# A retention block and a three-way maxout feed-forward on one core: the order of weight conversion, transposes and weight sums between the matmuls

## The chip, the cores and the metric

The kernel runs on one core of a Trainium2 chip. The metric is the device time of one execution in microseconds (us), as a median over several executions. The core has five engines, each of which works through its own instruction queue: TensorE (PE in the profile, with its weight loads as PEld), VectorE (DVE), ScalarE (ACT), GpSimd (POOL) and SyncE (SP). SyncE only issues DMAs here.

## What is computed

The reference, cut to what matters:

```python
# attention: batch 8, heads 8, sequence 576, head dimension 64, float32
scores = scale * np.matmul(q, k.transpose(0, 1, 3, 2))
gamma = 1.0 - 2.0 ** (-5.0 - np.arange(H, dtype=np.float32))
Dmat = np.where(rel >= 0, gamma[:, None, None] ** rel[None, :, :], 0.0)
attn = np.matmul(scores * Dmat, v)                       # rel = i - j
x = attn.transpose(0, 2, 1, 3).reshape(4608, 512)
# feed-forward: d_model 512, d_ff 768, weights given in float64
h = np.maximum(np.maximum(x @ w1, x @ w2), x @ w3)
out = h @ w_out
```

## The kernel before, in words

The 4608 tokens are cut into 36 chunks of 128 tokens, and four chunks make a block t of 512 tokens; there are nine blocks, 0 to 8. Attention is done chunk by chunk in its recurrent form: per chunk the kernel transposes q and k (`transposes`), multiplies them into scores and masks these (`scores`), multiplies keys by decayed values into a state (`state`, scaled and added in `keep`), and multiplies scores and old state with values and queries into the chunk's output (`values`, whose last step `output` writes xT, the transposed input of the feed-forward). Chunks up to 6 are transposed on TensorE and copied by ScalarE (L274, L275); from chunk 7 on VectorE transposes them (`kT`, `qT`, through `soon`).

The feed-forward of block t (`ffn(t)`) runs while the attention of block t+1 is woven into it: `steps(t+1)` is a list of twelve slots written out by hand, and the main loop does one slot's steps and then lets the feed-forward go on to its next `yield`.

The weights come in float64. `convert_all` is a generator that turns them into float32 with integer operations on VectorE and ScalarE. Each unit of two 128-row pieces goes through `exponent` (L632 on VectorE, L634 on ScalarE), `fraction` (L640, L641, L643), `whole` (L646), `sign` (L650) and `product` (L658), which writes the float32 weight and issues the load of a further piece on SyncE. `convert(n)` advances the generator by n of its stops. Units 0 to 2 go half by half; from unit 3 on both halves go together, and the exponent of unit n+1 comes ahead of the sign and product of unit n.

Block 0 uses the plain products: `up_plain` (L786) for each of three weight matrices and six 128-row groups of the hidden layer, in the order of `units`, which is three entries (matrices) for each pair fp of groups; then `downs_plain` (L773). The queue of VectorE is in the order of these calls, so `convert(n)` and the attention steps share it in the order in which they stand in the code.

Blocks 1 to 8 use a scheme with fewer multiplications. For each pair fp of hidden groups, a "hidden pair" (order 0, 2, 1), `up` (L762) makes 20 products of sums of x and sums of weights, accumulated in five matmul banks a to e; `after` copies them on ScalarE (L747, `part` or `h`) and joins them on VectorE (L750). A join is a sum or maximum; those named D2, B6 and A7 come three at a time at the end of a hidden pair. The sums of weights are made once in place, 19 per hidden pair (`weight_sums`, L470). The sums for pair 0 are made at the end of block 0, those for pairs 2 and 1 during block 1. `downs` (L559) is the output stage in seven products with the matrices T (from sums of the output weights) and S (hidden sums, `sums_of_hidden`: two on VectorE, L527 and L528, two on GpSimd, L529). The profile calls the first, third, fifth and seventh product dx, the second dy, the fourth and sixth dz; `To` are the buffers t1, t2 and t4 of the output weights' sums, and the fourth product (dz) uses b12, which is changed in place in `w_out`.

In blocks 1 to 8 two lists feed VectorE's queue between the matmuls: `urgent` (steps of the attention, the hidden sums, the loads; `soon` appends to it) and `chores` (weight sums). `chore(n)` takes n from `urgent`, or from `chores` if `urgent` is empty. Before the scores or values of a chunk everything in `urgent` is taken. In `ffn`, one of two branches is taken after each of the 40 steps of a hidden pair (L866 to L869): every fourth step takes one of `urgent` (also two steps later if `urgent` is long), and even steps take one of `chores`.

The lines that matter below: L203 (masks, xT and transposes that are done at once, without the list; the same at L196 from the list), L310 and L313 (scores sk and states kv of a chunk from 8 on), L345 (`state_factors`, a copy on ScalarE whose result GpSimd reads in L327), L512 and L513 (sums of the output weights on VectorE), L516 and L517 (the same on GpSimd), L880 (where these are put in the queues), L919 to L934 (the attention of block 0, in the order written out by hand).

Of the kernel before, what the change touches and what calls it, by code (L numbers as in the profile page):

```python
# [45 lines left out]
ALU = mybir.AluOpType  # L46
# [17 lines left out]
            b21 = b21 - b41, b42 = b42 - n5, b22 = b22 - b21, n6 = b31 + n2, b32 = b22 - b32, n8 = b12 - n4,  # L64
# [17 lines left out]
def kernel(  # L82
# [14 lines left out]
    nc = tc.nc  # L97
# [8 lines left out]
    CPT = NT // C  # L106
# [150 lines left out]
    def transposes(g):  # L257
        both = qks[g] = {}
        if g >= BY_CHUNKS:
            for n, tag in (("k", "kT"), ("q", "m1")):  # L260
                both[n] = att.tile([P, H, D], FP32, tag=tag, name=n + "T", bufs=2 if n == "k" else 3)
        else:
            both["k"] = att.tile([P, NP, C], FP32, tag="kT", name="kT", bufs=2)
            both["q"] = ppool.tile([P, NP, C], FP32, tag="part", name="qT")
        if g >= BY_PE:
            for n in ("k", "q"):
                soon(partial(nc.vector.transpose, both[n][:].rearrange("a p c -> a (p c)"),
                             raws.pop(("kx" if n == "k" else n, g))[:].rearrange("a x y i -> a (x y i)")))
            return
        for n, src in (("k", raws["k", g]), ("q", raws.pop(("q", g)))):  # L270
            pool, tag = (ps_r, "r") if g >= CPT else (ps_x, "x")
            pt = pool.tile([P, NP, C], FP32, tag=tag, name=n + "t")
            for p in range(NP):
                nc.tensor.transpose(pt[:, p, :], pair(src, p), ident[:C, :C])  # L274
            nc.scalar.copy(both[n][:], pt[:])  # L275

    def scores(g):
        chore(len(urgent))
        scale(len(scaling))
        if g >= BY_CHUNKS:  # L280
            chunk_scores(g)
            return
        qT, kT = qks[g]["q"], qks[g]["k"]
        s = [ps_r.tile([C, NP, C], FP32, tag="r", name=f"s{j}") for j in range(2)]
        for p in range(NP):
            for j in range(2):
                r = slice(D * j, D * (j + 1))
                nc.tensor.matmul(s[j][:, p, :], lhsT=kT[r, p, :], rhs=qT[r, p, :], start=True, stop=True)
        for j in range(2):
            st = sts[g, j] = att.tile([C, NP, C], FP32, tag=f"m{j}", name="st", bufs=2 + j)  # L290
            soon(partial(nc.vector.tensor_tensor, st[:], s[j][:],
                         masks[start_of(g)][:].unsqueeze(1).to_broadcast([C, NP, C]), op=ALU.mult))
# [50 lines left out]
    def state_factors():  # L343
        for j in range(2):
            nc.scalar.copy(gs_of[half(0), j::2], gs[half(j)])  # L345

    def state(g):

        kr = raws["k", g]
        kvs[g] = None  # L350
        if begins(g):
            r = start_of(g) or 0
            kvs[g] = ps_r.tile([P, NP, D], FP32, tag="r", name="kv")
            for h in range(H):
                nc.tensor.matmul(kvs[g][half(h % 2), h // 2, :], lhsT=kr[r:, h, :], rhs=vds[g][r:, h, :],
                                 start=True, stop=True)

    def keep(g):
        factor = gs[:].unsqueeze(2).to_broadcast([P, NP, D])

        def step(t, kv):
            if start_of(g) is not None:
                nc.vector.tensor_tensor(t[:], kv[:], factor, op=ALU.mult)
            else:
                nc.vector.tensor_tensor(t[:], kv[:], states[g][:], op=ALU.add)
                (nc.gpsimd if g < CPT - 2 else nc.vector).tensor_tensor(t[:], t[:], factor, op=ALU.mult)

        if begins(g):
            t = states[g + 1] = ppool.tile([P, NP, D], FP32, tag="part", name="state")
            soon(partial(step, t, kvs[g]))  # L370
# [133 lines left out]
    def sums_of_outs():  # L504

        pool = late["pool"]
        lo, hi = slice(0, DM // 2), slice(DM // 2, DM)
        b11, b12, b21, b22 = (w_out[:, :, e, r] for e in range(2) for r in (lo, hi))
        t1, t2, t4 = (pool.tile([P, NF // 2, DM // 2], FP32, name=f"To{n}")[:] for n in (1, 2, 4))

        def on_vector(fp):
            nc.vector.tensor_tensor(t1[:, fp], b12[:, fp], b11[:, fp], op=ALU.subtract)  # L512
            nc.vector.tensor_tensor(t2[:, fp], b22[:, fp], t1[:, fp], op=ALU.subtract)  # L513

        def on_gpsimd(fp):
            nc.gpsimd.tensor_tensor(b12[:, fp], b22[:, fp], b12[:, fp], op=ALU.subtract)  # L516
            nc.gpsimd.tensor_tensor(t4[:, fp], b21[:, fp], t2[:, fp], op=ALU.subtract)  # L517

        late["sums of T"] = [partial(on, fp) for on in (on_vector, on_gpsimd) for fp in (0, 2, 1)]
        late["T"] = {1: b11, 2: b21, 3: b22, 4: t4, 5: t1, 6: t2, 7: b12}  # L520
        late["S"] = {n: pool.tile([P, NF // 2, NH], FP32, name=f"H{n}") for n in (1, 2, 3, 4)}

# [201 lines left out]
    def late_room():  # L724
        pool = late["pool"]
        late["W"] = [pool.tile([P, NF, P], FP32, name=f"n{n}") for n in range(1, 9)]
        late["X"] = {n: pool.tile([P, NH], FP32, name=n)[:] for n in sorted({x[0] for x in X_SUMS})}
# [3 lines left out]
    def convert(n):  # L731
        for _ in range(n):
            next(converting, None)
# [84 lines left out]
    def ffn(t):  # L818

        h = hpool.tile([P, NF, NT], FP32, tag="h", name="h")  # L820
        if t == 0:
            for fp, i in units:
                if (fp, i) == units[0]:
                    first_ups(h)
                    yield
                    continue
                for fb in (2 * fp, 2 * fp + 1):
                    maximum, = up_plain(t, h, fb, i)
                    if (fp, i, fb) == (*units[1], 0):
                        scores(CPT)  # L830
                        state(CPT)
                        keep(CPT)
                    if (fp, i) == units[-1] and fb % 2:
                        maximum()
                        convert(2)
                    else:
                        convert(4 if (fp, i) == units[1] else 2)
                        maximum()
                yield
            convert(3)  # L840
            for fb, _ in enumerate(downs_plain(t, h)):
                convert(2 if fb < 2 else 4 * len(pieces))
                if fb == 2:
                    while_converting.close()
                    late["pool"] = ctx.enter_context(tc.tile_pool(name="late", bufs=1))
                    late_room()
                    sums_of_outs()
                    weight_sums(0)
                elif fb == 3:
                    chore(len(chores))  # L850
                if fb in (1, 3):
                    yield
            yield
            return
        order = (0, 2, 1)
        if t == 1:
            spread.append(True)
            weight_sums(2)
            weight_sums(1)
        total = len(order) * 2 * len(PRODUCTS)  # L860
        count = parts = 0
        for fp in order:
            while fp not in summed_fp:
                chore()
            for step, _ in enumerate(up(t, h, fp)):
                if step % 4 == 1 or step % 4 == 3 and len(urgent) > (2 if t == 1 else 6):  # L866
                    chore(len(urgent) > 0)
                elif step % 2 == 0 and chores:
                    chores.popleft()()  # L869
                if step % 3 == 2:  # L870
                    scale()
                count += 1
                if count * (NF // 2 * 3) >= (parts + 1) * total:
                    parts += 1
                    yield
            sums_of_hidden(h, fp)
        chore(len(urgent))
        for n, _ in enumerate(downs(t, h, order)):
            if t == 1 and n == 0:
                for step in late["sums of T"]:  # L880
                    step()
            chore(4)
            scale(2)
            if n in (1, 3):
                yield
        yield
# [34 lines left out]
    decay(2)  # L921
    state(1)
    keep(1)
    values([1], [1])
    scores(2)
    convert(2)
    state(2)
    keep(2)
    convert(1)
    values([2], [2])  # L930
    transposes(CPT - 1)
    convert(1)
    state_factors()
    convert(2)  # L934
    decay(CPT - 1)
    scores(CPT - 1)
# [99 lines left out]
```

## Time and profile before

| | value |
|---|---|
| median of 3 executions | 753.45 us (753.13 to 753.48) |
| profiled execution: time, and span in the profile | 753.01 us, 751.3 us |
| TensorE busy | 743.1 us (99% of the span) |
| TensorE weight loads busy | 615.1 us (82%) |
| VectorE busy | 518.7 us (69%) |
| ScalarE busy | 327.3 us (44%) |
| GpSimd busy | 71.4 us (10%) |
| DMA | 59.31 MB, 79 GB/s over the span, 232 GB/s over the first 60 us |
| TensorE clock granted | 1.0 |

Busy times are of one profiled execution; the end of a matmul is modelled, so a busy TensorE is not TensorE at its peak, and a short wait can hide in a modelled end. In time the span falls into three stretches: attention of block 0 with the first weights (to about 22 us), block 0's plain feed-forward beside the conversion (to 123.81 us, where block 1's first matmul e starts), and blocks 1 to 8, of which block 1 still makes sums of weights. The loads are crowded at the start: the first 60 us move 13.94 MB of the 59.31.

### The profile page before, as it was taken

What the parts mean: (1) busy time and instruction counts of PE and PEld (TensorE: products, weight loads), DVE (VectorE), ACT (ScalarE), POOL (GpSimd) and SP (SyncE); (2) the same over time, 40 slices, a digit from 0 to 9 for tenths busy, and PEclk for the clock granted to TensorE, in tenths of its full rate; (3) what the DMA queues carried; (4) which work ended last, traced back from release to release, by engine and by line L of the source; (5) the groups of instructions that cost most, each with busy time, mean ns of one, the idle gap of its engine ahead of it and who ended that gap; (6) DMA issues with size and microseconds to landing.
All of it is one profiled execution on the core that took longest, in us unless ns stands there. A gap on an engine that the chain in (4) does not pass through costs nothing.

```text
span 751.3 us, 16659 instructions
## 1 busy us (share of the span) xinstructions
PE 743.1 (99%) x6768; PEld 615.1 (82%) x6768; DVE 518.7 (69%) x878; ACT 327.3 (44%) x657; POOL 71.4 (10%) x91
## 2 busy tenths in 40 slices
PE   9999999999999999999999999999999999999998
PEld 7645546888788888888888888888888888888887
DVE  3898899898846765686667746775667656763662
ACT  3764533554145433644254335542554255414441
POOL 3000000002300100011010101010101010100000
PEclk9999999999999999999999999999999999999999
DMA  9996842504252514241333224242514151000001
GB/s 229 239 226 140 225 92 72 99 12 85 62 94 41 100 37 96 48 81 48 80 77 68 61 66 90 35 81 67 102 24 91 44 94 35 2 29 29 1 0 57
DMA packets 230206, 59.31 MB, mean 79 GB/s; under 512 B 210801, under 2 KB 228849, under 8 KB 230129
## 3 DMA queue, kind: packets, MB, share of 16 engines
q1 hardware_dynamic: 228720, 57.91, 35.6%
q8 instruction: 53, 0.87, 0.5%
q10 hardware_dynamic: 1408, 0.33, 0.2%
q14 instruction: 25, 0.20, 0.1%
HBM read 48.76 MB, written 9.44 MB: 77 GB/s over the span
## 4 chain that ended last, share of the span: by engine, by line
PE 90%; DVE 6%; SPq 2%; DMA 1%; issue 1%; ACT 0%; POOL 0%; DVEq 0%; POOLq 0%
PE a L762 18%; PE b L762 15%; PE dx L559 11%; PE c L762 8%; PE up L786 6%; PE dz L559 6%; PE d L762 5%; PE e L762 5%; PE sk L310 3%; PE down L773 3%; PE dy L559 2%; PE o L427 2%; PE o L434 1%; DVE part L750 1%; SPq L241 1%; DVE h L750 1%
## 5 line engine op out<-in xcount | busy, mean ns | idle before, releaser
L750 DVE TENSOR_TENSOR part<-part 128x512 f32<-128x512 f32 x168 | 116.0, 690 | 104.5 <-ACT part L747 102.0
L747 ACT COPY part<-b 128x512 f32<-128x512 f32 x120 | 70.3, 586 | 151.8 <-PE b L762 151.4
L750 DVE TENSOR_TENSOR h<-h,part 128x512 f32<-128x512 f32 x120 | 83.7, 698 | 29.5 <-ACT h L747 25.1
L747 ACT COPY part<-a 128x512 f32<-128x512 f32 x96 | 56.3, 586 | 51.2 <-PE a L762 50.8
L762 PE MATMUL a<-s,w 128*128 128x256 f32 x288 | 73.9, 379 | 0.0
L762 PE MATMUL b<-s,n 128*128 128x256 f32 x288 | 73.9, 379 | 0.0
L191 ACT ACTIVATE vraw<-vraw,gk 128x64 f32<-128x64 f32 x208 | 65.4, 346 | 0.5 <-DMA vraw<-in_v_dram 0.4
L786 PE MATMUL up<-xT,w 128*128 128x512 f32 (+2 forms) x160 | 64.2, 554 | 1.0 <-DVE w L658 1.0
L762 PEld LDWEIGHTS a<-s,w 128*128 128x128 f32 x288 | 54.7, 190 | 7.4
L762 PEld LDWEIGHTS b<-s,n 128*128 128x128 f32 x288 | 54.7, 190 | 7.4
L786 PEld LDWEIGHTS up<-xT,w 128*128 128x128 f32 x160 | 28.5, 190 | 31.3 <-issue 26.7
L327 POOL TENSOR_TENSOR s<-s,gs_of 64x512 f32<-64x512 f32 x21 | 22.3, 1062 | 318.1 <-DVE s L325 161.8
L762 PE MATMUL c<-xT,w 128*128 128x256 f32 x192 | 51.3, 389 | 0.0
L762 PE MATMUL d<-s,w 128*128 128x256 f32 x192 | 49.8, 380 | 0.0
L529 POOL TENSOR_TENSOR H<-h 128x256 f32<-128x256 f32 x24 | 20.2, 844 | 309.7 <-DVE h L750 305.3
L762 PE MATMUL b<-xT,n 128*128 128x256 f32 x192 | 49.3, 379 | 0.0
L559 PE MATMUL dx<-To,H 128*128 128x256 f32 (+1 forms) x204 | 45.4, 371 | 1.0 <-DVE To L513 1.0
L762 PE MATMUL e<-xT,w 128*128 128x256 f32 x192 | 45.4, 379 | 0.0
L762 PE MATMUL a<-xT,n 128*128 128x256 f32 x192 | 45.4, 379 | 0.0
L559 PEld LDWEIGHTS dx<-To,H 128*128 128x128 f32 x204 | 36.5, 190 | 6.6 <-DVE To L513 1.8
L762 PEld LDWEIGHTS e<-xT,w 128*128 128x128 f32 x192 | 36.5, 190 | 5.4 <-issue 0.5
L762 PEld LDWEIGHTS a<-xT,n 128*128 128x128 f32 x192 | 36.5, 190 | 5.0
(124 smaller groups left out, 1291.8 us busy)
## 6 DMA issues: line engine op xcount, KB each, us to landing
bits<-in_moe_w_dram SPq DMA_DIRECT2D x36, 256.0 KB, 6.0
out_dram<-osb SPq DMA_DIRECT2D x35, 256.0 KB, 2.1
kraw<-in_k_dram SPq DMA_DIRECT2D x32, 256.0 KB, 3.3
vraw<-in_v_dram SPq DMA_DIRECT2D x32, 256.0 KB, 3.9
qraw<-in_q_dram SPq DMA_DIRECT2D x224, 32.0 KB, 2.3
kxraw<-in_k_dram SPq DMA_DIRECT2D x224, 32.0 KB, 2.2
bits<-in_moe_w_out_dram SPq DMA_DIRECT2D x6, 512.0 KB, 5.5
qraw<-in_q_dram SPq DMA_DIRECT2D x6, 256.0 KB, 5.2
```

The source lines that it names most:

```text
L191: scaling.popleft()()
L241: nc.sync.dma_start(t[row:row + m], src[b, :, pos:pos + m, :].rearrange("h p d -> p h d"))
L310: nc.tensor.matmul(s[half(c), h, :], lhsT=kT[half(c), h, :], rhs=qT[half(c), h, :], start=True, stop=True)
L327: nc.gpsimd.tensor_tensor(new, new, factor, op=ALU.mult)
L427: nc.tensor.matmul(o[m][half(c), n, u, :], lhsT=vds[g][half(m), h, :], rhs=sts[g][half(m), h, :], start=n == 0 and u == 0, stop=place(g, m ...
L529: urgent.append(lambda: (pool(s3, a11, a21, op=ALU.subtract), pool(s4, a12, s2, op=ALU.subtract)))
L559: nc.tensor.matmul(o, lhsT=hS[n](fp)[:, m * P:(m + 1) * P], rhs=late["T"][n][:, fp, cols], start=first and fp == order[0] and (m == 0 or l ...
L747: nc.scalar.copy(of[step], ps[step[0]][:])
L750: nc.vector.tensor_tensor(of[dst], a, b, op=op)
L762: nc.tensor.matmul(ps[chain][:, e, :], lhsT=factor(w, 2 * fp + e), rhs=xS[t][x], start=n == 1 and e == 0, stop=ends, skip_group_check=True)
L773: nc.tensor.matmul(b[:], lhsT=h[:, fb, m * P:(m + 1) * P], rhs=w_sb["out", fb], start=(fb == 0), stop=(fb == NF - 1))
L786: nc.tensor.matmul(ps[:, a:b], lhsT=w_sb[i, fb][:, dc * P:(dc + 1) * P], rhs=xT[t][:, dc, a:b], start=dc == 0 and a == 0, stop=dc == NDC - ...
```

## The change

Six edits in the order of instructions:

- The sums of the output weights that GpSimd did (b12, t4) are now done by VectorE. The twelve sums are ordered by step (t1 for pairs 0, 2, 1; then t2; then b12; then t4). The first six are put in the queue after the first product of block 1's output stage, the other six after the third.
- In block 0's second unit, the scores, state and keep of chunk 4 are called after the conversion steps and the maximum, not ahead of them.
- `state_factors` is called at the end of block 0's output stage instead of in the attention of block 0.
- In blocks 1 to 8 every step of a hidden pair that takes none of `urgent` takes one of `chores`, not only the even steps.
- In the attention of block 0, the conversion steps stand elsewhere: two ahead of chunk 1's values (the exponent and fraction of the first half of the first weights), two after chunk 3's transposes (the whole of that half, then its sign and product), and two after chunk 2's values (exponent and fraction of the second half).
- The transposes of chunk 3 stand ahead of chunk 2's values.

The diff:

```diff
@@ -508,15 +508,9 @@
-        def on_vector(fp):
-            nc.vector.tensor_tensor(t1[:, fp], b12[:, fp], b11[:, fp], op=ALU.subtract)
-            nc.vector.tensor_tensor(t2[:, fp], b22[:, fp], t1[:, fp], op=ALU.subtract)
-
-        def on_gpsimd(fp):
-            nc.gpsimd.tensor_tensor(b12[:, fp], b22[:, fp], b12[:, fp], op=ALU.subtract)
-            nc.gpsimd.tensor_tensor(t4[:, fp], b21[:, fp], t2[:, fp], op=ALU.subtract)
-
-        late["sums of T"] = [partial(on, fp) for on in (on_vector, on_gpsimd) for fp in (0, 2, 1)]
+        sums = ((t1, b12, b11), (t2, b22, t1)), ((b12, b22, b12), (t4, b21, t2))
+        late["sums of T"] = [partial(nc.vector.tensor_tensor, *(x[:, fp] for x in step), op=ALU.subtract)
+                             for steps in sums for step in steps for fp in (0, 2, 1)]
@@ -826,16 +820,16 @@
                     maximum, = up_plain(t, h, fb, i)
-                    if (fp, i, fb) == (*units[1], 0):
-                        scores(CPT)
-                        state(CPT)
-                        keep(CPT)
                     if (fp, i) == units[-1] and fb % 2:
                         maximum()
                         convert(2)
                     else:
                         convert(4 if (fp, i) == units[1] else 2)
                         maximum()
+                    if (fp, i, fb) == (*units[1], 0):
+                        scores(CPT)
+                        state(CPT)
+                        keep(CPT)
@@ -843,6 +837,7 @@
                     late["pool"] = ctx.enter_context(tc.tile_pool(name="late", bufs=1))
+                    state_factors()
                     late_room()
@@ -865,7 +860,7 @@
                 if step % 4 == 1 or step % 4 == 3 and len(urgent) > (2 if t == 1 else 6):
                     chore(len(urgent) > 0)
-                elif step % 2 == 0 and chores:
+                elif chores:
                     chores.popleft()()
@@ -876,8 +871,8 @@
         for n, _ in enumerate(downs(t, h, order)):
-            if t == 1 and n == 0:
-                for step in late["sums of T"]:
+            if t == 1 and n in (0, 2):
+                for step in late["sums of T"][3 * n:3 * n + 6]:
                     step()
             chore(4)
@@ -921,16 +916,14 @@
     decay(2)
     state(1)
     keep(1)
+    convert(2)
     values([1], [1])
     scores(2)
-    convert(2)
     state(2)
     keep(2)
-    convert(1)
+    transposes(CPT - 1)
+    convert(2)
     values([2], [2])
-    transposes(CPT - 1)
-    convert(1)
-    state_factors()
     convert(2)
     decay(CPT - 1)
     scores(CPT - 1)
```

## The prediction

> **What bounds the kernel now.** I read the page's busy times first. TensorE is busy 743.1 of 751.3 us, so nothing on another engine matters unless TensorE waits for it, and the change reorders a few matmuls without adding or removing one. I therefore read next the list of what TensorE waited for (engine and line, releaser: us in total, times, longest).
>
> ```profile
> PE warm L158 <- POOL ident masks.py:199: 1.4, 1, 1.4
> PE dx L559 <- DVE To L513: 1.0, 2, 0.6
> PE up L786 <- DVE w L658: 1.0, 1, 1.0
> PE sk L310 <- DVE qT L196: 0.9, 1, 0.9
> PE s L288 <- ACT qT L275: 0.7, 1, 0.7
> PE o L396 <- DVE st L203: 0.3, 2, 0.2
> ```
>
> Apart from the start, which the change leaves, five waits of 3.9 us in all are everything that could be won. Then the timeline of TensorE, to place each (start, us, what, idle before it):
>
> ```profile
> 50.11 7.13 PE L786 MATMUL up<-xT,w 128*128 128x512 f32 x16 [1.03 <-DVE w L658]
> ...
> 170.93 0.33 PE L310 MATMUL sk<-qT,kT 64*64 64x64 f32 x3 [0.85 <-DVE qT L196]
> ...
> 190.75 1.13 PE L559 MATMUL dx<-To,H 128*128 128x256 f32 x4
> 192.31 1.13 PE L559 MATMUL dx<-To,H 128*128 128x256 f32 x4 [0.44 <-DVE To L513]
> 194.04 1.13 PE L559 MATMUL dx<-To,H 128*128 128x256 f32 x4 [0.60 <-DVE To L513]
> 195.01 1.24 PE L559 MATMUL dz<-w_out,H 128*128 128x256 f32 x5
> ...
> 271.13 1.13 PE L559 MATMUL dx<-To,H 128*128 128x256 f32 x4
> ...
> 273.82 1.46 PE L559 MATMUL dz<-w_out,H 128*128 128x256 f32 x6
> ```
>
> Idle times understate a stall, because the end of a matmul is modelled. I price stalls start to start: from the first dx on To to the first dz is 195.01-190.75 = 4.26 us in block 1 and 273.82-271.13 = 2.69 in block 2, so this stall costs 1.57, not 1.04. Likewise the last hidden pair of block 1 (first matmul e at 162.78, first dx of the output stage at 183.45) takes 20.67, against 19.49 for the same pair in block 2 (244.34 to 263.83): the sk stall costs 1.18. Check: block 1 from e to e is 205.37-123.81 = 81.56, block 2 is 284.19-205.37 = 78.82; the difference of 2.74 is 1.57+1.18. From 205 us on TensorE has no wait.
>
> **What the Trainium skill says.** "Perfetto Trace Analysis", section on the Tensor Engine instruction: TensorE's end time is an estimate and ScalarE, VectorE and GpSimd are strict first in, first out. The trace agrees: the 1.57 against 1.04 above. "SBUF — State Buffer", section "SBUF: two separate sides": VectorE (with two SBUF inputs) and GpSimd share a port pair by an exclusive lock; the loser blocks for the whole instruction. The trace agrees, in VectorE's and GpSimd's timelines:
>
> ```profile
> 189.25 0.41 DVE L512 TENSOR_TENSOR To<-w_out 128x256 f32<-128x256 f32 x1
> 189.69 0.83 DVE L513 TENSOR_TENSOR To<-w_out,To 128x256 f32<-128x256 f32 x1
> 190.45 0.94 DVE L512 TENSOR_TENSOR To<-w_out 128x256 f32<-128x256 f32 x1
> 191.43 0.83 DVE L513 TENSOR_TENSOR To<-w_out,To 128x256 f32<-128x256 f32 x1
> ```
>
> ```profile
> 189.40 0.84 POOL L529 TENSOR_TENSOR H<-h,H 128x256 f32<-128x256 f32 x1 [0.36 <-DVE H L528]
> 190.21 0.90 POOL L516 TENSOR_TENSOR w_out<-w_out 128x256 f32<-128x256 f32 x1
> 191.07 0.90 POOL L517 TENSOR_TENSOR To<-w_out,To 128x256 f32<-128x256 f32 x1
> ```
>
> Alone, a VectorE sum takes 0.41; beside GpSimd it ends 0.28 us after GpSimd's instruction ends (190.24 and 190.52, 191.11 and 191.39, 191.97 and 192.26).
>
> **The change, part by part.**
>
> *Output weights' sums (L512 to L523).* The six GpSimd instructions (0.90 each) become VectorE ones, and VectorE does t1 of all three pairs, then t2, then b12 and t4 one stage later. Hs2 ends and t1 of pair 0 starts at 189.25 as before. The next t1 is blocked by GpSimd's H sum, which stays, until 190.24, and ends at 190.52. After that nothing contends, and VectorE's starts are 0.335 apart (as in the weight sums at L470, 110.31, 110.64, 110.98): the third t1 starts at 190.45, t2 of pair 0 at 190.79, ending about 191.20; pair 2 ends at 191.54, pair 1 at 191.87. TensorE wants pair 0 at 190.75 and then one pair each 0.86 us, so it waits about 0.5 once and never again. Gain 1.57-0.5 = 1.07. Bounds: 1.57 if the second t1 isn't blocked, 0.8 if one more is. b12: VectorE follows with the first output's sum (0.60), so b12 of pair 0 ends near 192.8; dz needs it at 191.25+2.6 = 193.9. The six added VectorE instructions (2.0 us) push block 1's xT and x sums to about 194.4, where they start today at 194.51, and VectorE then has 2.67 us of idle before its 200.46 instruction. If that cover were gone, block 2 would wait for the x sums.
>
> *More weight sums per step (L868).* I counted out the order in which block 1's loop takes from its two lists. Today pair 2's 19 sums are taken in the first hidden pair and pair 1's 19 in the second. With the change nine of pair 1's move into the first hidden pair and the rest are out by step 12 of 40 of the second. In the first VectorE has 1.13+0.89+0.29+0.76 = 3.07 us of idle before the D2 joins at 141.52, waiting for ScalarE; it takes the six extra sums up to there in them. From there four more sums (1.34 us) lie ahead of the join that reads matmul e's bank: it ends near 153.9 instead of 152.55. Matmul d needs the bank at 154.51, so it is still 0.6 early. From step 12 of the second pair twelve sums (4.0 us) no longer follow, which lets VectorE catch up: the xT outputs and kT run by 160.4, the D2 joins start when ScalarE is done (160.98), and counted on with today's spacings (2.17 joins, 0.63 qT, 1.92 joins, 0.63 kT, 2.08 joins, 0.70) the late qT ends at 169.2, today 170.87. TensorE wants it at 169.85. The sk stall goes whole: gain 1.18; 0.5 if VectorE stays 0.65+0.7 us later than counted.
>
> *The start (L919 to L934).* Exponent and fraction of the first weights go ahead of chunk 1's outputs, chunk 3's transposes ahead of chunk 2's values. The first weights' bits landed by 14.5 (ScalarE's first conversion starts there); VectorE's two instructions (0.42 each) fit before xT at 15.45. The transposes fill TensorE's wait for the masks (2 x 0.16) and their copies run while the values are multiplied, so the 0.73 goes too; the first up-product could start at about 21.2, for 22.19. SP's order of DMAs is unchanged; q of chunk 3 (issued 11.78, 5.7 us to landing) is there at 17.5, just when wanted. But this 1.0 us meets the wait at 50.11, which hangs on DMAs:
>
> ```profile
> 46.37 0.68 DVE L791 TENSOR_TENSOR h<-h,up 128x512 f32<-128x512 f32 x1
> 46.97 0.69 DVE L632 TENSOR_SCALAR expo<-bits 128x1024 int32<-128x1024 int32 x1
> ```
>
> *Masks of chunk 4 after the conversion (L829).* This brings VectorE's weight chain forward by 1 to 2 us. The weights wanted at 50.11 (unit 3) come from two loads that land at 42.44 (issued 35.74, 6.7 us to landing). But VectorE takes the exponent of the next unit ahead of unit 3's sign and product, and that next unit's last load was issued at 38.41 with 8.3 us to landing: 46.71. The queue is full (DMA busy 9 tenths from 3 us on), so I leave this landing where it is. Then exponent 46.73, sign 0.60 later, product 1.26 after it, taking 1.23: 49.82, TensorE at 49.87 for 50.11. Gain 0.24; the other 0.8 us only lengthens TensorE's wait. Bounds: 0 if the load lands 0.25 later, 1.3 if it lands early enough for TensorE or the sign step to be last.
>
> *State factors (L345) moved:* two ScalarE copies (0.41 together) go to the block-0 output stage, where ScalarE is idle for 16.03 us before 121.43; their first reader is at 144.54. Cost nothing.
>
> Sum: 0.24+1.18+1.07 = 2.49 us. The profiled execution took 753.01 (span 751.3 and 1.7 around it), so 750.5; it lies 0.44 under the median, which gives 753.45-2.5 = 750.95, say 750.9.
>
> **Rivals.** *The start pays as well.* TensorE and VectorE free the early buffers sooner, SP issues sooner, the last load lands 1 us earlier: gain 3.5 to 3.8, 749.8. For it: DMA traffic dips to 183 GB/s at 26 to 28 us. Against: the issues there take 0.6 us each and show no wait for an engine. *A gap only shrinks.* VectorE is later than counted at qT, or the lock takes two instructions at t2: gain 1.2, 752.2. Against: the trace confirms each duration. *Slower.* The extra sums hold VectorE up in the second hidden pair until matmul d waits for matmul e's bank. The margin is 0.6 us; each sum more ahead of it costs 0.34 and each sum that meets GpSimd's H sum 0.9. Past the margin every us is TensorE's, and from 0.6+2.5 = 3.1 us of extra lag the whole is slower: at 4.5 us, 754.9 or more. For it: VectorE has no idle from 141.5 to 170. Against: nine sums of 0.34 would have to be misplaced.
>
> **How the numbers follow.** The forecast has 0.63 (750.2 to 751.7), start pays 0.15, a gap shrinks 0.15, slower 0.07. About 1.5 us (0.2%) is what can be told from no change, so faster means under 751.95. Faster: 0.63+0.15, and a little of the third, 0.81; same 0.13; slower 0.06. Range 749.6 to 752.2.
>
> **What would show it.** In the changed trace the wait of sk for qT is gone; dx for To is one wait near 0.5 or less; the wait of up for w stays and grows to 1.5 to 2 us with its product ending near 49.8; d doesn't wait in the second hidden pair; the waits before 22 us are gone; block 1 takes about 79.3 us from e to e. A wait of d or dz on VectorE, or the up-product later than 50.1, would make the forecast wrong.

## The result and the profile after

| | before | after |
|---|---|---|
| median of 6 executions each | 753.41 us (753.00 to 753.48) | 750.00 us (749.58 to 750.77) |
| ratio, 95% interval | | 0.9957, 0.9944 to 0.9970 |
| profiled execution: time, span | 753.01 us, 751.3 us | 749.71 us, 748.0 us |
| first matmul e of block 1, of block 2 | 123.81, 205.37 us | 122.67, 202.06 us |
| block 1 from e to e | 81.56 us | 79.39 us |
| from block 2's e to the end of the span | 545.93 us | 545.94 us |

The change makes the kernel 3.4 us faster; the interval of the ratio stands for 2.3 to 4.2 us. Of the 3.31 us by which block 2 starts earlier, block 1 gives 2.17 and the stretch ahead of it 1.14. After that nothing differs.

The list of what TensorE waited for in the changed kernel (engine and line, releaser: us in total, times, longest), which answers to the first list of the prediction:

```profile
PE warm L158 <- POOL ident masks.py:199: 1.4, 1, 1.4
PE qt L274 <- DMA qraw<-in_q_dram: 1.1, 1, 1.1
PE dx L553 <- DVE To L876: 0.5, 1, 0.5
```

Four of the waits of before are gone (up for w, sk for qT, s for qT, o for st), that for To has shrunk from two to one, and one is new: the transposes of chunk 3 wait for q. TensorE's timeline of the changed kernel shows where (start, us, what, idle before it):

```profile
19.09 0.63 PE L274 MATMUL qt<-ident,qraw 128*128 128x128 f32 x4 [1.08 <-DMA qraw<-in_q_dram]
...
42.21 13.90 PE L780 MATMUL up<-xT,w 128*128 128x512 f32 x32
...
122.67 1.89 PE L756 MATMUL e<-xT,w 128*128 128x256 f32 x8
...
189.03 2.83 PE L553 MATMUL dx<-To,H 128*128 128x256 f32 x12 [0.53 <-DVE To L876]
191.70 2.75 PE L553 MATMUL dz<-w_out,H 128*128 128x256 f32 x12
...
202.06 1.89 PE L756 MATMUL e<-xT,w 128*128 128x256 f32 x8
```

The second line is one run of 32 matmuls: units 2 and 3 follow each other without a gap, where TensorE waited 1.03 us at 50.11 before. VectorE's timelines show why, and the two late edits beside it. First the kernel before, the product of unit 3 and the late qT:

```profile
48.83 1.23 DVE L658 TENSOR_TENSOR w<-mant,expo 128x1024 f32<-128x1024 f32 x1
...
170.17 0.70 DVE L196 STREAM_TRANSPOSE qT<-qraw 128x512 f32<-128x512 f32 x1
```

Then the changed kernel:

```profile
45.76 0.69 DVE L626 TENSOR_SCALAR expo<-bits 128x1024 int32<-128x1024 int32 x1 [0.84 <-DMA bits<-in_moe_w_dram]
46.37 1.22 DVE L644 SCALAR_TENSOR_TENSOR expo<-bits,expo 128x1024 int32<-128x1024 int32 x1
47.62 1.23 DVE L652 TENSOR_TENSOR w<-mant,expo 128x1024 f32<-128x1024 f32 x1
...
167.17 0.70 DVE L196 STREAM_TRANSPOSE qT<-qraw 128x512 f32<-128x512 f32 x1
...
186.93 1.61 DVE L876 TENSOR_TENSOR To<-w_out 128x256 f32<-128x256 f32 x3
188.47 1.08 DVE L876 TENSOR_TENSOR To<-w_out,To 128x256 f32<-128x256 f32 x3
```

VectorE now stands ready at the exponent of unit 4 (L626, L632 before) and waits 0.84 us for the load. The load landed at 45.63 and the exponent started at 45.76, so unit 3's product started at 47.62, where it was 48.83 before. The late qT ended at 167.87 (170.87 before). t1 of three pairs took 1.61 us in all and t2 followed.

### The profile page after: what moved, and what is told of

Its sections match the earlier page's. It is cut to its first block, busy times and chain, and to the rows that moved or that the text cites. A ratio compares the mean times of both kernels' runs of the same rounds, so it can differ in the third digit from the quotient of the medians.

```text
span 748.0 us, 16662 instructions
## 1 busy us (share of the span) xinstructions
PE 742.1 (99%) x6768; PEld 615.2 (82%) x6768; DVE 518.5 (69%) x884; ACT 327.1 (44%) x657; POOL 69.3 (9%) x85
## 4 chain that ended last, share of the span: by engine, by line
PE 97%; DVE 1%; DMA 1%; issue 0%; ACT 0%; POOL 0%; POOLq 0%; DVEq 0%
PE a L756 19%; PE b L756 17%; PE dx L553 11%; PE c L756 9%; PE up L780 8%; PE d L756 6%; PE dz L553 6%; PE e L756 6%; PE sk L310 3%; PE down L767 3%; PE dy L553 2%; PE o L427 2%; PE o L434 2%; PE s L288 1%; DMA qraw<-in_q_dram 1%; PE o L396 1%
## 5 line engine op out<-in xcount | busy, mean ns | idle before, releaser
L756 PEld LDWEIGHTS b<-xT,n 128*128 128x128 f32 x192 | 36.5, 190 | 5.0
```

What stands on the lines that cost most here:

```text
L756: nc.tensor.matmul(ps[chain][:, e, :], lhsT=factor(w, 2 * fp + e), rhs=xS[t][x], start=n == 1 and e == 0, stop=ends, skip_group_check=True)
```

## The experiments

Two questions: what each part is worth, and what sets the stretch ahead of block 1, where the result went past the forecast. In all twelve runs "block 1" is the time from its first matmul e to block 2's, which has the same length in every profile of the same late code. The last column is the gain of the medians minus the gain in block 1 (against 81.56), that is, what the edits ahead of block 1 gave.

| run | median, executions | before, same chip | ratio, 95% | block 1 | gain in block 1 | gain ahead of it |
|---|---|---|---|---|---|---|
| changed kernel | 750.00, 6 | 753.41 | 0.9957 (0.9944 to 0.9970) | 79.39 | 2.17 | 1.24 |
| e1_sums_even | 751.24, 9 | 753.13 | 0.9974 (0.9964 to 0.9984) | 80.54 | 1.02 | 0.87 |
| e2_outs_before | 751.25, 13 | 753.13 | 0.9977 (0.9968 to 0.9985) | 80.37 | 1.19 | 0.69 |
| e3_start_before | 749.94, 5 | 753.13 | 0.9960 (0.9947 to 0.9972) | 79.37 | 2.19 | 1.00 |
| e4_masks_before | 750.72, 11 | 753.13 | 0.9971 (0.9962 to 0.9980) | 79.37 | 2.19 | 0.22 |
| e5_early_only | 753.05, 13 | 753.34 | 0.9994 (0.9986 to 1.0002) | 81.57 | 0 | 0.29 |
| e6_sign_first | 750.09, 5 | 753.34 | 0.9952 (0.9939 to 0.9964) | 79.39 | 2.17 | 1.08 |
| e7_outs_in_pair | 751.86, 11 | 753.34 | 0.9980 (0.9971 to 0.9989) | 80.63 | 0.93 | 0.55 |
| e8_both | 751.00, 5 | 753.34 | 0.9964 (0.9950 to 0.9977) | 80.63 | 0.93 | 1.41 |
| e9_t1_in_pair | 750.13, 5 | 753.18 | 0.9952 (0.9940 to 0.9965) | 78.81 | 2.75 | 0.30 |
| e10_t1_sign_first | 748.89, 5 | 753.18 | 0.9941 (0.9929 to 0.9954) | 78.81 | 2.75 | 1.54 |
| e11_load_later | 749.29, 5 | 753.18 | 0.9945 (0.9931 to 0.9958) | 78.81 | 2.75 | 1.14 |
| e12_late_only | 751.11, 7 | 753.18 | 0.9971 (0.9961 to 0.9982) | 79.38 | 2.18 | -0.11 |

Block lengths come from one profile each and agree to 0.02 us where the late code is the same. The executions of one changed kernel lie 0.9 to 3.4 us apart, so a single value of the last column is rough.

### One part undone at a time

*Weight sums on even steps only.*

```diff
-                elif chores:
+                elif step % 2 == 0 and chores:
```

> The changed kernel with the weight sums taken only in even steps again. If the sk wait was cured by the sums' new places (forecast), the wait of sk for qT comes back, block 1 is 1.2 us longer from its first e to block 2's (80.6 instead of 79.4), and the time is 751.2. If the cure came from elsewhere (an earlier start of block 1, or GpSimd's sums leaving), block 1 stays at 79.4 and the time at 750.0.

The wait of sk for qT is back (0.9 us in the kernel before):

```profile
PE sk L310 <- DVE qT L196: 0.8, 1, 0.8
```

Block 1 is 1.15 us longer than in the changed kernel. The edit is worth 1.15 us.

*Output weights' sums as before*: GpSimd does b12 and t4, all twelve after the first product.

```diff
-            if t == 1 and n in (0, 2):
-                for step in late["sums of T"][3 * n:3 * n + 6]:
+            if t == 1 and n == 0:
+                for step in late["sums of T"]:
```

> The changed kernel with the output weights' sums as before (half of them on GpSimd, all put in the queue at once). Forecast: two waits of dx for To come back and the one of 0.53 goes; first dx on To to first dz is 4.26 instead of 3.2 or so, time 751.1. Rival, that GpSimd's part doesn't matter and only the order of t1 and t2 does: can't be told apart here, but if the time stays at 750.0 the whole item is worth nothing.

TensorE's timeline of this run has the two waits of before, and 4.25 us from the first dx on To to dz (194.17-189.92), as against 2.67 in the changed kernel (191.70-189.03):

```profile
189.92 1.13 PE L559 MATMUL dx<-To,H 128*128 128x256 f32 x4
191.48 1.13 PE L559 MATMUL dx<-To,H 128*128 128x256 f32 x4 [0.43 <-DVE To L513]
193.21 1.13 PE L559 MATMUL dx<-To,H 128*128 128x256 f32 x4 [0.60 <-DVE To L513]
194.17 2.11 PE L559 MATMUL dz<-w_out,H 128*128 128x256 f32 x9
```

Block 1 is 0.98 us longer. The difference of the two spacings is 1.58, but in the changed kernel 0.53 of wait lies ahead of the first dx, where the spacing leaves it out; 1.05 remains, near the 0.98. This run undoes three things together, the engine of the sums, their order and their split over two places; what each is worth alone was not tried.

*The order of the start as before* (the last part of the change's diff undone, with `state_factors` left late), and *the masks of chunk 4 ahead of the conversion as before* (the second part undone).

> The changed kernel with block 0's attention in the order of before (conversion steps and chunk 3's transposes), the rest changed. Theory A (the wait at unit 3 was the only gate, and the masks' move opened it): the start's order is worth nothing, block 1's first e starts within 0.3 us of 122.7, time 750.0. Theory B (the start's order is worth what it saves on TensorE, as its waits before 22 us are gone): e starts at 123.5 or later, time 750.8 to 751.

> The changed kernel with chunk 4's scores, state and keep ahead of the conversion again. Theory A (VectorE's chain to unit 3's weights was the gate): the wait of up for w comes back with about 1 us, e starts at 123.6, time 750.9. Theory B (as forecast, the last load of the next unit is the gate, with landing at 46.7 in either kernel): the move is worth 0.25, e starts at 122.9, time 750.2.

Without the new order of the start nothing is lost in the median: it is 3.19 us faster than before, and the gain ahead of block 1 is 1.0. The profiled execution, the slowest of the five at 750.67 us, came out as theory B has it, because unit 4's load held the exponent until 46.81, and the first e started at 123.65, not near 122.7. Without the masks' move 0.22 is left of the gain ahead of block 1. By these medians it is the masks' move that pays in this stretch, and not the order of the start. The intervals of the two ratios overlap, so the profiles must bear it out.

They do. With the masks moved, VectorE is early and waits for unit 4's load in all seven profiles in which that load's exponent stands ahead of unit 3's product (0.81 to 1.09 us). Without the move it reaches that exponent 24.8 us after the first up-product: 46.97-22.19 before, 46.92-22.07 in e12_late_only, without a wait in either. In e4_masks_before it is 24.8 us too, but there the first up-product happened to start at 21.18, so VectorE was early and waited 0.55 us, as its timeline shows:

```profile
46.56 0.70 DVE L626 TENSOR_SCALAR expo<-bits 128x1024 int32<-128x1024 int32 x1 [0.55 <-DMA bits<-in_moe_w_dram]
```

So this one profile doesn't have the masks as its gate. With the up-product at 22.19 VectorE would come at 47.0 again, as before (an estimate from these figures).

The aim of the start's order was the first up-product. It started at 22.19 before, at 22.35 in e3_start_before and at 22.07 in e12_late_only, which have the old order. With the new one it started at 22.36 in the changed kernel, and in all eleven profiles between 21.18 and 22.73, with a median of 22.19: on the whole, nothing. In each of them TensorE waits for a load of the attention instead, 0.18 to 1.58 us: for q of chunk 3 (the changed kernel, e1, e5, e7, e8, e11) or for the values of chunk 2, vd, which GpSimd makes from a load (e2, e4, e6, e9, e10). A wait for vd occurs with the old order too (e3 0.91, e12 0.57).

### The two ends alone

*Only the start, the masks and the state factors; the late edits undone.*

> The kernel before with the start's order, the masks' move and the state factors' move alone; the weight sums and the output weights' sums as before. Theory A (the change's first 124 us are gated by the landing of the next unit's last load, which differs from execution to execution between 45.7 and 47.3 us, and before could not use an early landing because its VectorE came to that exponent only at 46.97): 0.7 to 1.0 us faster than before in the median, with a wider spread than before, block 1 at 81.5. Theory B (the start is worth what the record said): 0.24 faster.

0.3 us faster, with an interval that takes in no change; the expectation was too high. Block 1 has its old length. In this profile the load for unit 4 was late (the exponent started at 47.18), and it shows 1.2 us of waits for q and 1.1 for k.

*Only the late edits and the state factors; start and masks as before* (the diff is against the changed kernel; the lines of the masks that it takes out further down are left out here).

```diff
+                    if (fp, i, fb) == (*units[1], 0):
+                        scores(CPT)
+                        state(CPT)
+                        keep(CPT)
                     if (fp, i) == units[-1] and fb % 2:
...
-    convert(2)
     values([1], [1])
     scores(2)
+    convert(2)
     state(2)
     keep(2)
+    convert(1)
+    values([2], [2])
     transposes(CPT - 1)
-    convert(2)
-    values([2], [2])
+    convert(1)
```

> The kernel before with the two late edits (weight sums at more steps, output weights' sums on VectorE) and the place of the state factors; start and masks as before. Theory: early and late stretches don't touch, so the late gain stands alone: block 1 in 79.4 us, 2.2 us faster (-2.0 to -2.3), and all times within about 1 us of each other, as with the kernel before, since VectorE's late arrival at the next unit's exponent (about 47.0) covers the landing. Rival: the parts need each other, and it is less than 1.8 us faster or spreads like the changed kernel.

2.07 us faster, 2.18 of it measured in block 1; the seven executions lie within 0.95 us, as those of the kernel before do (0.5 to 1.6 us in the four sets). The two ends don't touch. VectorE reaches the exponent of unit 4 at 46.92 without waiting, TensorE starts unit 3 at 50.06: the kernel before, in this stretch, to 0.05 us.

### What sets unit 3

In every profile in which TensorE waits for w at unit 3 and unit 4's exponent stands ahead, its start is 3.14 us after that exponent's (exponent, sign, product):

| | unit 4's exponent starts | unit 3 starts on TensorE | difference |
|---|---|---|---|
| before | 46.97 | 50.11 | 3.14 |
| e2_outs_before | 47.31 | 50.45 | 3.14 |
| e3_start_before | 46.81 | 49.95 | 3.14 |
| e4_masks_before | 46.56 | 49.71 | 3.15 |
| e5_early_only | 47.18 | 50.32 | 3.14 |
| e7_outs_in_pair | 45.87 | 49.00 | 3.13 |
| e9_t1_in_pair | 46.87 | 50.01 | 3.14 |
| e12_late_only | 46.92 | 50.06 | 3.14 |

From unit 3's start to block 1's first e it is 73.70 us in these profiles (123.81-50.11; 123.71-50.01; 123.41-49.71). So one bound on the first e is the start of unit 4's exponent plus 3.14+73.70 = 76.84 us. The other is TensorE's own arrival: where it doesn't wait at unit 3 (the changed kernel, e8, e10, e11), the first e comes 100.3 us after the first up-product (122.67-22.36, 122.91-22.59, 122.21-21.89, 122.88-22.56). The later of the two bounds gives the first e to 0.01 us in all ten profiles with unit 4's exponent ahead. In the changed kernel they are 122.60 by the load and 122.68 by the start, in e1_sums_even (exponent at 45.68, up-product at 22.12) 122.52 and 122.44: both so close together that no wait at unit 3 is listed.

In all but the kernel before and e12_late_only the exponent is held by the last load of unit 4. It starts 0.12 or 0.13 us after the landing, at 45.68 to 47.31, with a mean of 46.5 over the eight profiles. Where this is the later bound, each tenth of the landing is a tenth of the result.

*Sign and product of a unit ahead of the next unit's exponent*, to take unit 4's load out of unit 3's way:

```diff
-            if following:
-                following.exponent(both)
             two.sign(both)
             yield
             two.product(both)
+            if following:
+                following.exponent(both)
```

> The changed kernel with the sign and product of a unit ahead of the next unit's exponent. Theory A (that exponent, which waits for the next unit's last load, holds up the product): unit 3's product ends near 48.2 whatever the landing, the wait of up for w is under 0.3, e starts at 122.3 to 122.8, 0.5 us or so faster than the changed kernel in the median (so 3.7 faster than before) with a narrower spread. Theory B (TensorE's own start is the gate): nothing moves, 3.2 faster than before.

In part: unit 3's product no longer waits for unit 4's load, but in this execution TensorE still waited 0.48 us for the product, as the exponent of unit 3 itself was held by its load until 43.45, and 1.58 us at the start for vd. The first e came at 123.25, later than expected. Over the four runs with this edit (e6, e8, e10, e11) the gain ahead of block 1 is 1.08, 1.41, 1.54 and 1.14, mean 1.29. Over the six without it that have both early edits (the changed kernel, e1, e2, e5, e7, e9; 57 executions) the mean by executions is 0.62. That puts the edit at about 0.7 us. Means of the single executions instead of medians give 1.50 and 0.64, thus 0.9 us with a standard error of 0.15. The intervals of two single runs, e9 and e10 for instance, still overlap.

### The wait that the change left

*All twelve sums of the output weights as chores in block 1's last hidden pair* (fp 1), and *this with the sign first*.

```diff
+            if t == 1 and fp == 1:
+                chores.extend(late["sums of T"])
...
-            if t == 1 and n in (0, 2):
-                for step in late["sums of T"][3 * n:3 * n + 6]:
-                    step()
```

> The changed kernel with the twelve sums of output weights taken as chores in hidden pair 1, ahead of the output stage. If the 0.53 wait of dx for To that is left comes from GpSimd's H sum blocking the second t1 (forecast), it goes, and first dx on To to first dz is 2.7 as in block 2: 0.5 us faster than the changed kernel. If the sums delay the masks, the joins or the x sums instead, a new wait of d, sk or e of block 2 takes its place and the time is the same or more.

> Both edits of the two kernels above together. If they are independent, their gains add: 1.0 us faster than the changed kernel, 4.2 faster than before.

The gains don't come: the sums delay the joins, as the first expectation allows, and both runs lose 1.24 us in block 1. The wait for To is gone, and another has come. TensorE's timeline of e7_outs_in_pair:

```profile
184.60 1.13 PE L553 MATMUL dx<-w_out,h 128*128 128x256 f32 x4 [1.55 <-DVE h L744]
```

The output stage's first product waits for the hidden values of pair 1: twelve sums held up the joins that make them. How much room there is shows in VectorE's timeline of the changed kernel, at the D2 joins of that pair:

```profile
179.36 2.14 DVE L744 TENSOR_TENSOR part<-part 128x512 f32<-128x512 f32 x3 [2.64 <-ACT part L741]
```

The next run has *only the three t1 sums there*, and the one after it *the sign first as well*:

```diff
+            if t == 1 and fp == 1:
+                chores.extend(late["sums of T"][:3])
...
-                for step in late["sums of T"][3 * n:3 * n + 6]:
+                for step in late["sums of T"][3 if n == 0 else 6:3 * n + 6]:
```

> The changed kernel with only the three t1 sums of the output weights taken as chores in the second of block 1's hidden pairs to run (pair 1 in name is the last; the sums are put into the list as the last pair begins); t2 stays at the output stage. Theory: three sums are 1.0 us of VectorE, less than its 2.6 us of idle time ahead of that pair's D2 joins, so nothing is late, and at the output stage t2 of pair 0 follows the H sums at once. The wait of dx for To (0.53) goes; first dx on To to first dz is 2.7 us; block 1 takes 78.85 us from e to e for 79.39; 0.5 us faster than the changed kernel, -3.7 us against before. Rival: three sums delay the joins as six did, h of pair 1 comes late, dx waits for h (1.55 us with six), and block 1 takes 79.4 or more: no gain, -2.5 to -3.2.

> The same, and the sign and product of a unit of first weights ahead of the next unit's exponent. Theory: two independent gains; no wait of the up-product of unit 3 for the next unit's load, and block 1 in 78.85 us: -4.2 us against before, of which 0.5 over the changed kernel is from block 1 and up to 0.5 from the start. Rival: the early gain is lost to the landing of q of chunk 3 or v of chunk 2: then -3.7.

VectorE's timeline of e9_t1_in_pair:

```profile
177.90 0.69 DVE L744 TENSOR_TENSOR part<-part 128x512 f32<-128x512 f32 x1
180.40 2.15 DVE L744 TENSOR_TENSOR part<-part 128x512 f32<-128x512 f32 x3 [1.81 <-ACT part L741]
...
187.97 1.62 DVE L878 TENSOR_TENSOR To<-w_out,To 128x256 f32<-128x256 f32 x3
```

After the three sums VectorE still waits 1.81 us for ScalarE ahead of the D2 joins, so nothing is late; t2 follows the hidden sums at once, and the first dx on To starts without a wait. Block 1 takes 78.81 us, the length of block 2. The expected 78.85 is met, and e9 as a whole only in part: 3.05 us for 3.7. Its profiled execution, near the median, has unit 4's exponent at 46.87 and so the first e at 46.87+76.84 = 123.71. With the sign first as well, the median is 748.89 us, 4.3 under the kernel before, as expected, and the lowest of all. TensorE's list of waits in that run:

```profile
PE warm L158 <- POOL ident masks.py:199: 1.4, 1, 1.4
PE kv L355 <- POOL vd L252: 1.1, 1, 1.1
```

Only waits ahead of the first up-product are left.

*The load of chunk 5 after the next weights' loads.*

```diff
         convert(2)
+        load(CPT + 1)
         state(g)
...
-            at(0, (load, b))
```

> The same, and the load of q, k and v of chunk 5 issued after the first weights' loads of the next conversion rather than before. Theory: unit 3's own loads land about 3 us earlier, some 40 us, so TensorE never waits for w there and unit 3 starts when TensorE arrives, whatever the landing; q of chunk 5 then lands about 38.7 and is wanted at about 41.2. 0 to 0.4 us faster than without it. Rival: q or k of chunk 5 is late and its transposes make TensorE wait, or the slack that is won was not the last: 0 or slower by up to 2 us.

TensorE doesn't wait at unit 3 and not for q of chunk 5 either, but unit 3 hadn't waited in e10's profile without it, and 749.29 against 748.89 is no gain. This profile's first up-product is 0.67 us later than e10's, with a wait for q of chunk 3 (1.53) where e10 has one for vd (1.15), and its first e is 0.67 us later too. Both stand ahead of the edit. The edit isn't worth keeping on this evidence.

## Why the prediction was right, and where it was off

*Weight sums.* The prediction has 1.18; the run with them undone shows 1.15. VectorE caught up in the second hidden pair as it was counted: the late qT ended at 167.87, where the prediction's 169.2, less the 1.14 us by which block 1 starts earlier, is 168.1. The join that reads matmul e's bank ended at 152.75 where the count gave 153.9-1.14 = 152.8, and d didn't wait. The case "slower" was thus not near.

*Output weights' sums.* The prediction has 1.07 (1.57 less a wait of 0.5); measured 0.98 and one wait of 0.53. The count of the lock held to the hundredth: from the start of the first t1 to the end of t2 of pair 0 it gave 191.20-189.25 = 1.95 us, and the trace has 186.93 to 188.88 (188.47 and one sum of 0.41). b12, which dz needs, was never late.

*The start's order.* The prediction let it run out: the first up-product 1.0 us earlier, and that 1.0 lost again in the wait at 50.11. It was lost, but elsewhere and for another reason; that this term still came out right is luck. The step that failed is "q of chunk 3 (issued 11.78, 5.7 us to landing) is there at 17.5, just when wanted". q was issued at 12.05 in the changed kernel and was there at 19.0, 6.9 us later, and across the runs TensorE waited for q or for vd, so the up-product came no earlier on the whole. Two of the prediction's signs didn't come: not all waits before 22 us are gone, and the wait of up for w, which was to grow to 1.5 to 2 us, is gone in the profiled execution.

*The masks' move.* The mechanism is the prediction's: VectorE comes earlier to the exponent of unit 4, which stands ahead of unit 3's product, and that load is the new bound; the 3.14 us chain after it held in all eight profiles. The term that was mis-sized is the landing of 46.71: "I leave this landing where it is". It isn't a place but a spread, 45.6 to 47.2 from one execution to the next. The prediction's 0.24 became 1.14 in the profiled execution, whose load landed at 45.63, and about 0.6 over 57 executions. The prediction's own bounds for this term, 0 to 1.3, hold both.

*Whole.* With 2.17 for block 1 and 0.6 ahead of it the change is worth about 2.8 us; the first six executions showed 3.4. The forecast 2.5 lies in their interval, and 750.0 in its range. The rival "the start pays as well" came close to the time for a wrong reason. Its load did land 1.1 us earlier (45.63 for 46.72), but SyncE didn't issue it sooner: at 39.70, 1.3 us later than before (38.41). And undoing the start's order cost nothing (749.94). SyncE's DMA view has the time from this issue to the landing, first for the kernel before, then for the changed one:

```profile
bits<-in_moe_w_dram SPq DMA_DIRECT2D x1, 256.0 KB, 8.3
bits<-in_moe_w_dram SPq DMA_DIRECT2D x1, 256.0 KB, 5.9
```

*State factors.* In the prediction at no cost; they stand late in every run, so no run prices them alone. No wait for them shows.

*What stays open.* Why a load lands when it does. The DMAs ahead of the first changed instruction are already 0.25 us apart between the two profiles (the second k is issued at 3.48 before and 3.73 after), so a part is there whatever the order. Whether another order of the loads would bring q of chunk 3 and v of chunk 2 earlier, where 0.2 to 1.6 us of each new start goes, wasn't tried.

## What to carry to other kernels

A step that gains on a load's landing has no one price: work out the bound from the load and the bound from the engine that needs it, and give the term the spread of landings over several profiles rather than the landing of one. In an in-order queue, don't put an instruction that waits for the next tile's load ahead of the work that finishes the present one. And where sums must be fitted in before a deadline, count the idle time that stands ahead of the next join: three of 0.34 us went free into 2.6 us, twelve did not.

## What was not expected of the hardware

- The same load, in kernels whose loads are issued in the same order, landed between 45.56 and 47.18 us in eight profiles, 5.6 to 6.8 us after its issue. The kernel before mostly hides this because VectorE gets there only at 46.97, and its executions lie closer together than those of the changed kernels (27 of them within 1.3 us, e1's nine within 2.5). In the Trainium skill, "DMA: Bandwidth & Descriptors", section "Latency and other measured facts", has an access latency to the chip's main memory of 0.2 us on average and 2 us at high load. The times here are longer than either, with several loads under way at once; no run separates latency from waiting behind other loads.
- In both programs a DMA is issued only after the DMA eight issues earlier has landed, so one late landing can hold back the issues that follow. In the kernel before, SyncE's issues at 42.45, 43.55 and 44.63 come 0.02 to 0.07 us after such landings (42.43, 43.48 and 44.57).
- A hidden sum on GpSimd that takes 0.84 us in the kernel before (at 152.95) lasted 3.72 us while VectorE ran sums and joins without a break. GpSimd's timeline of the changed kernel:

```profile
149.68 0.84 POOL L523 TENSOR_TENSOR H<-h 128x256 f32<-128x256 f32 x1 [5.09 <-DVE h L744]
153.16 3.72 POOL L523 TENSOR_TENSOR H<-h,H 128x256 f32<-128x256 f32 x1 [2.64 <-DVE H L522]
```

No one waited for it here. It fits the lock that the prediction counts with, seen from the other side, but "Perfetto Trace Analysis", section "GPSIMD Engine Instruction", calls GpSimd's reported spans unreliable, and no run was made to tell the two apart.
